# Two inverse-transform row blocks from one PSUM bank each, and the row-block steps listed one by one

## The chip, the cores and the metric

The kernel runs on one core of a Trainium2 chip. The metric is the device time of one execution in microseconds (us). The median of three runs of the kernel before is 1539.2 us (1536.36 to 1539.36). The engines are named PE (matmuls; PEld for its weight loads), DVE (VectorE), ACT (ScalarE), POOL (GpSimd) and SP (SyncE, which issues DMAs).

## What is computed

The state `x` has 2048 rows of 512 columns in bf16. Two layer kinds alternate, twice each:

```python
def _A_ref(x, w_r, w_i):                      # spectral filter
    X = jnp.fft.rfft2(x.astype(jnp.float32), axes=(-2, -1)) * (w_r + 1j * w_i)
    return jnp.fft.irfft2(X, s=(S, D), axes=(-2, -1)).astype(jnp.bfloat16)
...
def _B_ref(x, wq, wk, wv, wo):                # 32 heads share one key and one value, 16 wide
    p = _softmax(scores, axis=-1)             # scores = q k^T / 4
    return (p @ v, heads joined) @ wo
...
x = x + _A_ref(_layernorm(x), A_w_r, A_w_i)
x = x + _B_ref(_layernorm(x), B_wq, B_wk, B_wv, B_wo)
x = x + _A_ref(_layernorm(x), A_w_r, A_w_i)
x = x + _B_ref(_layernorm(x), B_wq, B_wk, B_wv, B_wo)
```

A spectral layer with the attention layer behind it is called a pair here; there are two.

## The kernel before, in words

**Layout.** `x` stays on the chip as `x_sb` of 128 partitions x 4 (r) x 4 (t) x 512. A *block* t is the four rows r = 0..3 of each partition: sequence position 512 r + 4 p + t. One block holds 512 rows of the sequence.

**A pair's stages.** The front normalises the blocks and transforms them along the sequence; `middle` goes over the width, applies the filter and comes back over the width, which leaves the spectra `H` (odd wave numbers) and `G[0]` (even ones). `blocks`, which the change rewrites, does the last inverse transform over the sequence block by block, adds it to `x`, normalises the new rows and makes keys, values and the first queries from them. `run` is then the attention: 579 steps of exponentials on ACT (L672), a part of the exponentials as integer images on DVE and POOL (L706, L721, L725), scores and products on PE (L583, L685).

**The inverse transform of a block.** The four rows of a block at one partition are the sums and differences of two even parts and two odd parts. `odd(t)` (L347) computes the odd parts in a pair of PSUM banks with 16 matmuls and ACT copies them out as `bp` (L354). `even(t, i)` for i = 0, 1 (L365) computes each even part with eight matmuls, both parts in one pair of banks: four with the tables of multiples of four, which are the same for both i, and four with the tables of the other even numbers, which change sign between i = 0 and 1. `rows_out` (L382) adds and subtracts `bp` on DVE. For blocks 2 and 3 (`WITH_X`) PE adds the old `x` through identity matmuls (`old_rows`, L372), so that DVE writes `x_sb` at once; for blocks 0 and 1 DVE writes `dst` and then adds `x` (L384).

**From rows to keys.** `stats_rows` (L115, L119) gives mean and variance per row, `root` (L122) the square root on ACT, `scales` (L126, L127) the factors on DVE, `apply` the normalised rows `X_new` on ACT (L142) or DVE (L144). They reach the layout of the keys, `xz`, either by transposing DMAs on SP (`turned_rows`, L426; two per block, each for two rows) or by eight PE transposes and one copy (`transposed`, L418 and L421). `keys` (L435) then makes a block's keys: ACT casts them (L437) and DVE takes the largest absolute value (L438). `values` (L449) makes values, which ACT writes four times with different factors (L451). `first_queries` (L458), `qabs` (L409) and `ready` (L462 to L464) prepare the first queries with a bound that needs all four largest values.

**What sets the order.** In front, middle and blocks the instructions of PE, ACT and DVE run in the order in which the Python code issues them (`manual_schedule`); a new instruction that needs another engine's result waits on that engine's semaphore, and what stands behind it on its engine waits too. In `blocks` before, the order is: block t's odd and even matmuls, then the `rows_out` of it, with statistics and normalising of block t-1 after the matmuls of block t+1. Blocks 0 and 1 are normalised on ACT and transposed by DMA (four DMAs in a pair), blocks 2 and 3 are normalised on DVE and transposed on PE. A dummy exponential (L1071) loads ACT's table for the attention before the last transposes.

**PSUM.** In this stage three pairs of banks (tag p2) hold the odd and even parts, keys and queries, and two single banks (tag mm) values and transposes. In pair 0 of the kernel before, the single banks are the first to be placed; in pair 1 the pairs are. The attention that follows puts its scores in the first five banks.

Of the kernel before, what the change touches and what calls it, by code (L numbers as in the profile page):

```python
# [12 lines left out]
P = 128  # L13
# [23 lines left out]
WITH_X = (2, 3)  # L37
# [3 lines left out]
def host_tables():  # L41
# [40 lines left out]
    tabs["IE"], tabs["IO"] = bf(ie), bf(io)  # L82
# [108 lines left out]
class Spectral:  # L191
# [149 lines left out]
    def odd(self, t):  # L341
        IO, ps = self.tabs["IO"], self.big()
        for i in range(2):
            for c in range(2):
                h = self.H[:, t % 2, c, :, :]
                for ab in range(2):
                    self.mm(ps[:, i, :], lhsT=IO[:, turned(c, t, ab, i * ab), t, :], rhs=h[:, i ^ ab, :], start=(c == 0 and ab == 0), stop=(c == 1 and ab == 1 and t not in WITH_X))  # L347
# [6 lines left out]
        self.nc.scalar.copy(out=bp_new, in_=ps)  # L354
        self.bp[t] = bp_new

    def even(self, t, i):
        IE = self.tabs["IE"]
        if i == 0:
            self.pair[t] = self.big()  # L360
        ps = self.pair[t]
        for c in range(4):
            for ab in range(2):
                tab = IE[:, 0, 2 * c + ab, t, :] if c < 2 else IE[:, 1, turned(c - 2, t, ab, i), t, :]
                self.mm(ps[:, i, :], lhsT=tab, rhs=self.G[0][:, c, ab, :], start=(c == 0 and ab == 0), stop=(c == 3 and ab == 1 and t not in WITH_X))  # L365
        if t in WITH_X:
            self.old_rows(ps, t, i, False)
# [6 lines left out]
    def rows_out(self, t, us=(0, 1), parts=(slice(0, 2),)):  # L374

        ps, bp, x = self.pair[t], self.bp[t], self.x_sb[:, :, t, :]
        dst = x
        if t not in WITH_X:
            dst = self.work.tile([P, 4, 512], BF, tag="m", bufs=3, name="dst")
        for u in us:  # L380
            for i in parts:
                self.tt(out=dst[:, 2 * u:2 * u + 2, :][:, i, :], in0=ps[:, i, :], in1=bp[:, i, :], op=(ALU.add, ALU.subtract)[u])  # L382
        if t not in WITH_X:
            self.tt(out=x, in0=dst, in1=x, op=ALU.add)  # L384


class Attention:
# [25 lines left out]
    def transposed(self, psum, t, xn, half, engine):  # L413

        ps = psum.tile([P, 2, NC, P], BF, tag="mm", bufs=2)
        for i in range(2):
            for c in range(NC):
                self.nc.tensor.transpose(ps[:, i, c, :], xn[:, 2 * half + i, c * P:(c + 1) * P], self.tabs["EYE"][:, 0, :])  # L418
        k = 4 * t + 2 * half
        copy = engine.copy if engine is self.nc.scalar else engine.tensor_copy  # L420
        copy(out=self.xT[:, k:k + 2, :, :], in_=ps)  # L421
# [6 lines left out]
    def keys(self, psum, t, last=False):  # L428

        nc, aw = self.nc, self.aw  # L430
        k0, k1 = 4 * t, 4 * t + 4
        two = psum.tile([P, 2, 512], F32, tag="p2", bufs=3)
        ps = two[:, 0, 0:(k1 - k0) * P]
        for c in range(NC):
            nc.tensor.matmul(ps, lhsT=aw["wk"][:, c, :], rhs=self.xT[:, k0:k1, c, :],  # L435
                             start=(c == 0), stop=(c == NC - 1))
        cast = lambda: nc.scalar.activation(out=self.KT[:, k0 * P:k1 * P], in_=ps, func=ACT.Identity, bias=self.tabs["KAB"][:, 1:2], scale=self.tabs["KAB"][:, 0:1])  # L437
        bound = lambda: nc.vector.tensor_reduce(out=self.kmax[:, t:t + 1], in_=ps, axis=mybir.AxisListType.X, op=ALU.max, apply_absolute_value=True)  # L438
        if last:
            bound()  # L440
        cast()
        return bound

    def values(self, psum, t):
# [5 lines left out]
        for j in range(4):  # L450
            nc.scalar.mul(out=aw["vaug"][:, j, 4 * t:4 * t + 4, 0:DH], in_=psv, mul=PH_W[j])  # L451
# [7 lines left out]

    def ready(self):  # L460
        nc, kq, qt = self.nc, self.kq, self.QT[0]
        nc.vector.tensor_reduce(out=kq[:, 0:1], in_=self.kmax, axis=mybir.AxisListType.X, op=ALU.max)  # L462
        nc.vector.tensor_scalar(out=kq[:, 1:2], in0=kq[:, 0:1], scalar1=self.tabs["KAB"][:, 2:3], scalar2=self.tabs["KAB"][:, 0:1], op0=ALU.mult, op1=ALU.add)
# [322 lines left out]
def full_kernel(ctx, tc, A_x, A_w_r, A_w_i, B_x, B_wq, B_wk, B_wv, B_wo, out, n_pairs=2):  # L786
# [222 lines left out]
    def blocks(work, sp, psum, att):  # L1009
        A, D = nc.scalar, nc.vector  # L1010

        def put(t, X, engines, rows=range(R)):
            for r, engine in zip(rows, engines):
                norm.apply(engine, x_sb[:, r, t, :], X[:, r, :], r, t)

# [4 lines left out]
        def sums(t):  # L1020
            for i in range(2):
                sp.even(t, i)

        def stats(t, rows=range(R)):
            norm.stats_rows(x_sb[:, :, t, :], t, rows)

        def rows_turned(t, engines):
            norm.scales(t)
            X = new_rows()
            for half in range(2):  # L1030
                put(t, X, engines[2 * half:2 * half + 2], (2 * half, 2 * half + 1))
                att.turned_rows(t, X, half)

        sp.odd(0)
        sums(0)
        sp.rows_out(0, parts=(slice(0, 1), slice(1, 2)))
        sp.odd(1)
        sums(1)
        stats(0)
        norm.root(0)  # L1040
        sp.rows_out(1)
        sp.odd(2)
        sums(2)
        rows_turned(0, (A,) * 4)
        stats(1)
        norm.root(1)
        sp.rows_out(2)
        sp.odd(3)
        sums(3)
        rows_turned(1, (A,) * 4)  # L1050
        bound0 = att.keys(psum, 0)
        stats(2)
        norm.root(2)
        sp.rows_out(3, (0,))
        stats(3, (0, 1))
        norm.root(3, slice(0, 2))
        sp.rows_out(3, (1,))
        norm.scales(2)
        xn2 = new_rows()
        put(2, xn2, (D,) * 4)  # L1060
        att.values(psum, 0)
        norm.scales(3, slice(0, 2))
        xn = new_rows()
        put(3, xn, (D, D), (0, 1))
        att.transposed(psum, 2, xn2, 0, A)
        att.transposed(psum, 2, xn2, 1, A)
        bound1 = att.keys(psum, 1)
        stats(3, (2, 3))
        norm.root(3, slice(2, 4))
        dmyo = small.tile([P, 1], F32, tag="dmyo", bufs=1)  # L1070
        nc.scalar.activation(out=dmyo, in_=norm.eps, func=ACT.Exp)  # L1071
        att.transposed(psum, 3, xn, 0, A)
        query = att.first_queries(psum)
        bound0()
        att.values(psum, 1)
        norm.scales(3, slice(2, 4))
        put(3, xn, (D, D), (2, 3))
        bound1()
        bound2 = att.keys(psum, 2)
        att.transposed(psum, 3, xn, 1, D)  # L1080
        query()
        bound2()
        att.keys(psum, 3, True)
        att.qabs(att.QT[0])
        att.values(psum, 2)
        att.values(psum, 3)

    last, inverse = None, {}
    for pair in range(n_pairs):
        with ExitStack() as es:  # L1090
# [8 lines left out]
            for name in ("IO", "IE"):  # L1099
# [97 lines left out]
```

## Time and profile before

| | us |
|---|---|
| median of three runs | 1539.2 |
| profiled execution, its own time | 1539.34 |
| span in its trace (first to last instruction) | 1537.6 |
| mean granted TensorE clock | 0.984 of full speed |
| pair 0: first sum of the spectra (L339) / first exponential (L672) | 69.77 / 115.49 |
| pair 1: the same | 827.11 / 870.21 |
| pair 0: first `rows_out` of blocks 0, 1, 2, 3 | 79.43, 85.95, 92.47, 98.42 |
| pair 1: the same | 834.98, 841.50, 848.03, 853.98 |

A row of the page's list of groups reads: line, engine, operation, out<-in with partitions x elements and type, xcount | busy us, mean ns of one | idle us of the engine just before, and what ended it. A row of the timeline reads: start, length, engine, line, operation, count, and in brackets the idle time before it with its releaser. The table of stretches gives, for each stretch of time, its length and the busy us (and number) of PE, PEld, DVE, ACT and POOL, then the granted clock of TensorE, the share of the DMA engines and GB/s. The chain of waits lists, in order of time, the work that ended last.

### The profile page before, as it was taken

To read this page: it belongs to the slowest core of one execution; us is meant where nothing else is said; L and a number is where in the kernel's file an instruction comes from. 1 tells how busy PE (TensorE), PEld (TensorE's weight loads), DVE (VectorE), ACT (ScalarE), POOL (GpSimd) and SP (SyncE) were. 2 spreads that over 40 slices of the span, in tenths; PEclk is the share of its full clock that TensorE was granted. 3 is DMA by queue.
4 is the path that set the end of the run, shared out by engine and by line. 5 is a ranking of instruction groups with operands and counts; after the bars stand their busy time and mean duration, and the time that the engine had idled before them with its cause. 6 is when DMAs were issued, how large, how long until landed. Compare 5 with 4: busy or idle time off the path is not lost.

```text
span 1537.6 us, 33033 instructions
## 1 busy us (share of the span) xinstructions
PE 1350.1 (88%) x13181; PEld 432.3 (28%) x13220; DVE 1418.2 (92%) x2273; ACT 1436.7 (93%) x1359; POOL 778.3 (51%) x1310
## 2 busy tenths in 40 slices
PE   5888888899889988999889788888998899889987
PEld 2442222222222222222235322222222222222222
DVE  6688999999999999999987889999999999999996
ACT  6649999999999999999965799999999999999997
POOL 1004555555556555655610055555556655565555
PEclk9997999999999999999999899999999999999999
DMA  8110000000000000000010100000000000000000
GB/s 286 17 28 1 2 2 1 1 1 2 1 2 1 1 1 2 1 2 1 2 42 1 28 1 2 1 1 5 1 5 4 5 5 5 5 4 5 5 5 18
DMA packets 21791, 19.51 MB, mean 13 GB/s; under 512 B 14212, under 2 KB 19076, under 8 KB 21380
## 3 DMA queue, kind: packets, MB, share of 16 engines
q1 hardware_dynamic: 21252, 16.35, 3.5%
q8 instruction: 103, 1.69, 0.5%
q0 software_dynamic: 384, 1.05, 0.2%
q14 instruction: 52, 0.43, 0.1%
HBM read 13.20 MB, written 2.10 MB: 10 GB/s over the span
## 4 chain that ended last, share of the span: by engine, by line
ACT 34%; DVE 34%; issue 14%; PE 14%; POOL 0%; DVEq 0%; POOLq 0%; ACTq 0%
ACT e L672 33%; DVE t_new L706 17%; DVE s_new L721 9%; PE pv_new L685 3%; PE sc L583 3%; PE new L365 2%; DVE o L602 2%; PE new L216 1%; DVE qt L405 1%; DVE ot_new L623 1%; PE dv L583 1%; PE new L347 1%; PE new L255 1%; PE new L311 1%; DVE qt L409 1%
## 5 line engine op out<-in xcount | busy, mean ns | idle before, releaser
L672 ACT ACTIVATE e<-sc 128x1536 bf16<-128x1536 f32 (+1 forms) x1158 | 1313.7, 1298 | 5.4 <-PE dv L583 3.3
L725 POOL TENSOR_SCALAR pool_new<-t_new 128x512 int16<-128x512 int16 x1204 | 727.6, 626 | 717.6 <-DVE s_new L721 629.6
L706 DVE TENSOR_SCALAR t_new<-dv 128x512 uint16<-128x512 f32 x1204 | 790.0, 678 | 58.9 <-PE dv L583 50.7
L685 PE MATMUL pv_new<-e,vaug 128*32 128x512 bf16 x2892 | 586.1, 388 | 0.0
L583 PE MATMUL sc<-qt,KT 32*128 32x512 bf16 x2892 | 457.5, 386 | 117.2 <-ACT e L672 110.6
L583 PE MATMUL dv<-qt,KT 32*128 32x512 bf16 x1204 | 453.2, 386 | 18.7 <-DVE t_new L706 15.7
L685 PE MATMUL pv_new<-s_new,vaug 128*32 128x512 bf16 x2408 | 427.4, 386 | 6.4 <-DVE s_new L721 6.2
L721 DVE TENSOR_SCALAR s_new<-t_new 128x3584 int16<-128x3584 int16 (+1 forms) x380 | 392.8, 1034 | 0.1
L583 PEld LDWEIGHTS <-KT 32*128 32x128 bf16 x4096 | 156.2, 91 | 559.5 <-issue 555.1
L685 PE MATMUL pv_new<-pool_new,vaug 128*32 128x512 bf16 x1204 | 302.2, 385 | 1.3 <-POOL pool_new L725 1.3
L685 PEld LDWEIGHTS <-vaug 128*32 128x32 bf16 x7708 | 156.1, 94 | 379.8 <-issue 348.4
L685 PE MATMUL pv_new<-t_new,vaug 128*32 128x512 bf16 x1204 | 231.2, 385 | 0.3
L399 PE MATMUL ps<-xz,wq_sb 128*128 128x512 bf16 x248 | 65.2, 386 | 1.0 <-DVE t_new L706 0.8
L602 DVE STREAM_TRANSPOSE o<-pv_new 128x512 f32<-128x512 f32 x64 | 45.3, 707 | 7.3 <-PE pv_new L685 7.3
L216 PE MATMUL new<-tab_F,xz 128*128 128x512 bf16 x186 | 48.3, 405 | 3.6 <-DVE xz L180 3.3
L405 DVE TENSOR_SCALAR qt<-ps,kq 128x512 bf16<-128x512 f32 x62 | 46.0, 742 | 1.2 <-PE ps L399 1.2
L617 POOL TENSOR_TENSOR od_new<-o,den 128x256 bf16<-128x256 f32 x62 | 38.4, 620 | 0.0
L115 DVE BATCH_NORM_STATS2 st<-x_sb 128x6 f32<-128x512 bf16 x48 | 31.1, 674 | 3.9 <-DMA x_sb<-in_A_x_dram 3.7
L280 DVE TENSOR_TENSOR m<-x_new,wt 128x1024 bf16<-128x1024 bf16 x32 | 20.7, 688 | 14.3 <-ACT x_new L256 14.3
L256 ACT CAST x_new<-new 128x1024 bf16<-128x1024 f32 x16 | 16.2, 1012 | 18.4 <-PE new L255 17.0
L399 PEld LDWEIGHTS <-wq_sb 128*128 128x128 bf16 x256 | 22.4, 98 | 32.4 <-issue 17.8
L365 PE MATMUL new<-G_new,t_new 128*128 128x512 bf16 x128 | 29.9, 379 | 0.5 <-DVE G_new L332 0.4
(109 smaller groups left out, 586.8 us busy)
## 6 DMA issues: line engine op xcount, KB each, us to landing
tab_F<-const_F SPq DMA_DIRECT2D x5, 640.0 KB, 11.5
x_sb<-in_A_x_dram SPq DMA_DIRECT2D x4, 512.0 KB, 4.8
t_new<-const_IE SPq DMA_DIRECT2D x2, 1024.0 KB
rt<-in_A_w_r_dram SPq DMA_DIRECT2D x1, 1028.0 KB, 7.6
rt<-in_A_w_i_dram SPq DMA_DIRECT2D x1, 1028.0 KB, 11.8
t_new<-const_IO SPq DMA_DIRECT2D x2, 512.0 KB, 5.6
out_dram<-x_sb SPq DMA_DIRECT2D x8, 128.0 KB, 1.7
out_dram<-x_sb POOLq DMA_DIRECT2D x8, 128.0 KB, 2.1
```

Of the source, the lines that this page charges most:

```text
L216: self.mm(ps, lhsT=z, rhs=tab, start=start and i == 0, stop=stop and i == len(mms) - 1)
L365: self.mm(ps[:, i, :], lhsT=tab, rhs=self.G[0][:, c, ab, :], start=(c == 0 and ab == 0), stop=(c == 3 and ab == 1 and t not in WITH_X))
L399: self.nc.tensor.matmul(ps, lhsT=self.aw["wq"][:, c, hg, :], rhs=self.xT[:, 4 * qb:4 * qb + 4, c, :], start=(c == 0), stop=(c == NC - 1))
L405: self.nc.vector.tensor_scalar(out=qt, in0=ps, scalar1=self.kq[:, 1:2], scalar2=None, op0=ALU.mult)
L583: nc.tensor.matmul(dst, lhsT=KT[hs, kc * P:(kc + 1) * P], rhs=QT[g][hs, :], start=True, stop=True)
L602: nc.vector.transpose(out=o.rearrange("p c j -> p (c j)"), in_=ps)
L617: return engine.tensor_tensor(out=turned_od[g // 2][:, :, half], in0=o[:, :, 0:DH], in1=den.unsqueeze(2).broadcast_to([P, 16, DH]), op=ALU ...
L672: nc.scalar.activation(out=e[:, 0:na, :], in_=sc[:, 0:na, :], func=ACT.Exp, scale=SCALE)
L685: nc.tensor.matmul(pv[g][32 * h:32 * h + 32, :], lhsT=vaug[:, max(j, 0), kc, :], rhs=rhs, start=(first_pv[(g, h)] == u), stop=(last_pv[(g, ...
L706: nc.vector.tensor_scalar(out=tb[(g, b)][:, i, :], in0=dv, scalar1=T_MUL, scalar2=T_ADD, op0=ALU.mult, op1=ALU.add)
L721: image[0] = nc.vector.tensor_scalar(out=s_new[:, lo:nt, :], in0=src[:, lo:nt, :], scalar1=PH_OFF[i], scalar2=None, op0=ALU.add)
L725: pace(nc.gpsimd.tensor_scalar(out=sb[(g, b, 3)][:, i, :], in0=src[:, i, :], scalar1=1.0, scalar2=PH_OFF[3], op0=ALU.mult, op1=ALU.add))
```

## The change

1. **Blocks 0 and 1** (`HALVED`): the second even part is no longer computed with eight matmuls in a bank of its own. The first part is computed in one single bank; once DVE has taken its sum and difference with `bp`, four matmuls with a new table `IE2` (minus two times the sign-changing half, 128x3x2x128 bf16, loaded per pair) are added into the same bank, which turns it into the second part. `rows_summed(t, i)` takes sum and difference for one i, `rows_added` adds `x`.
2. **The steps of all four blocks** are issued one by one in a new order: `odd`, `keys` and `values` return their ACT copies as functions that are called later. Block 0's statistics come in two halves, and the DMAs and PE transposes are dealt out anew: blocks 0 and 1 by DMA (four), half of block 2 and half of block 3 by DMA (one each) and the other halves by PE. Block 2 is normalised on ACT, three of block 3's rows on DVE. The dummy exponential comes behind the last transposed copy; the values of blocks 2 and 3 are scaled ahead of the last key cast.
3. **The bound of the queries** is split: `bounds` reduces the first three blocks' largest values, `ready` brings in the fourth with a step that takes the larger of the two.
4. **Bank pairs first**: one unused pair is taken at the start of pair 0, so that the pairs are placed ahead of the single banks, as in pair 1.

```diff
+WITH_X, HALVED = (2, 3), (0, 1)
...
+tabs["IE2"] = bf(2 * ie[:, 1, 1:, :2])
...
     def even(self, t, i):
+        if t in HALVED:
+            if i == 0:
+                self.pair[t] = self.bank()
+            for c in range(2 * i, 4):
+                for ab in range(2):
+                    tab = self.tabs["IE2"][:, turned(c - 2, t, ab, 1) - 1, t, :] if i else IE[...]
+                    self.mm(self.pair[t], lhsT=tab, rhs=self.G[0][:, c, ab, :], start=(c == 0 and ab == 0), stop=(c == 3 and ab == 1), skip_group_check=True)
+            return
...
+    def rows_out(self, t, u):
+        self.tt(out=self.x_sb[:, 2 * u:2 * u + 2, t, :], in0=self.pair[t], in1=self.bp[t], op=(ALU.add, ALU.subtract)[u])
+    def rows_summed(self, t, i):
+        if i == 0:
+            self.dst = self.work.tile([P, 4, 512], BF, tag="m", bufs=3, name="dst")
+        for u in range(2):
+            self.tt(out=self.dst[:, 2 * u + i, :], in0=self.pair[t], in1=self.bp[t][:, i, :], op=(ALU.add, ALU.subtract)[u])
+    def rows_added(self, t, rows=slice(0, R)):
+        x = self.x_sb[:, rows, t, :]
+        self.tt(out=x, in0=self.dst[:, rows, :], in1=x, op=ALU.add)
...
+    def bounds(self):
+        self.nc.vector.tensor_reduce(out=kq[:, 0:1], in_=self.kmax[:, 0:NQB - 1], ...)
+        self.nc.vector.tensor_scalar(out=kq[:, 0:1], in0=kq[:, 0:1], scalar1=kab[:, 2:3], scalar2=kab[:, 0:1], op0=ALU.mult, op1=ALU.add)
     def ready(self):
+        nc.vector.tensor_scalar(out=kq[:, 1:2], in0=self.kmax[:, NQB - 1:NQB], ..., scalar2=kq[:, 0:1], op0=ALU.mult, op1=ALU.max)
...
                 if pair == 0:
+                    sp.big()
                     front_first(work, sp, psum, raw)
```

The new order in `blocks` (ACT is `A`, DVE is `D`):

```python
keep[0] = sp.odd(0); keep[0](); sp.even(0, 0); sp.rows_summed(0, 0); sp.even(0, 1); sp.rows_summed(0, 1)
sp.rows_added(0, slice(1, R, 2)); sp.rows_added(0, slice(0, R, 2)); stats(0, (0, 2))
sp.even(1, 0); keep[1] = sp.odd(1); stats(0, (1, 3)); keep[1](); sp.rows_summed(1, 0)
sp.even(1, 1); norm.root(0); sp.rows_summed(1, 1); keep[2] = sp.odd(2); norm.scales(0)
X[0] = new_rows(); sp.rows_added(1); sp.even(2, 0); put(0, 0, A); stats(1); sp.even(2, 1)
X[1] = new_rows(); put(0, 2, A); keep[3] = sp.odd(3); put(0, 1, A); keep[2](); norm.root(1)
sp.rows_out(2, 0); norm.scales(1); put(0, 3, A); att.turned_rows(0, X[0], 0); sp.even(3, 0)
att.turned_rows(0, X[0], 1); put(1, 0, A); sp.rows_out(2, 1); put(1, 3, A); stats(2, (2, 3)); keep[3]()
put(1, 1, A); sp.even(3, 1); stats(2, (0, 1)); X[2] = new_rows(); norm.root(2)
query = att.first_queries(psum); put(1, 2, A); att.turned_rows(1, X[1], 0); sp.rows_out(3, 0)
norm.scales(2); keys[0] = att.keys(psum, 0); put(2, 1, A); put(2, 2, A); X[3] = new_rows()
stats(3, (0, 1)); put(2, 0, A); put(2, 3, A); turned_out[2, 0] = att.transposed(psum, 2, X[2], 0)
sp.rows_out(3, 1); stats(3, (2, 3)); att.turned_rows(1, X[1], 1); norm.root(3, slice(0, 2))
values[0] = att.values(psum, 0); norm.scales(3, slice(0, 2)); att.turned_rows(2, X[2], 1)
keys[0][0](); norm.root(3, slice(2, 4)); norm.scales(3, slice(2, 4)); put(3, 0, D)
turned_out[2, 0](D.tensor_copy); put(3, 1, A); put(3, 3, D); keys[1] = att.keys(psum, 1)
put(3, 2, D); query(); values[0](); values[1] = att.values(psum, 1); att.turned_rows(3, X[3], 0)
keys[1][0](); values[1](); turned_out[3, 1] = att.transposed(psum, 3, X[3], 1); turned_out[3, 1](A.copy)
table_loaded(); keys[0][1](); keys[2] = att.keys(psum, 2); keys[1][1](); att.qabs(att.QT[0])
keys[3] = att.keys(psum, 3); keys[2][1](); att.bounds(); values[2] = att.values(psum, 2); keys[2][0]()
values[3] = att.values(psum, 3); values[2](); keys[3][1](); values[3](); keys[3][0]()
```

More of the change, by code (lines that the diff above doesn't have):

```diff
@@ L419, in transposed @@
         k = 4 * t + 2 * half
[L420 to L421 removed]
+        return lambda copy: copy(out=self.xT[:, k:k + 2, :, :], in_=ps)
     def turned_rows(self, t, xn, half):
@@ L1018, in new_rows, with put @@
             return X_new
-        def sums(t):
-            for i in range(2):
-                sp.even(t, i)
+        def put(t, r, engine):
+            norm.apply(engine, x_sb[:, r, t, :], X[t][:, r, :], r, t)
         def stats(t, rows=range(R)):
             norm.stats_rows(x_sb[:, :, t, :], t, rows)
[L1027 to L1032, printed above, removed]
@@ new lines, in blocks @@
+        X, keep, keys, values, turned_out = {}, {}, {}, {}, {}
+        keep[0] = sp.odd(0)
+        keep[0]()
+        sp.even(0, 0)
+        sp.rows_summed(0, 0)
+        sp.even(0, 1)
+        sp.rows_summed(0, 1)
+        sp.rows_added(0, slice(1, R, 2))
+        sp.rows_added(0, slice(0, R, 2))
+        stats(0, (0, 2))
+        sp.even(1, 0)
+        keep[1] = sp.odd(1)
+        stats(0, (1, 3))
+        keep[1]()
+        sp.rows_summed(1, 0)
+        sp.even(1, 1)
+        norm.root(0)
@@ new lines, in blocks @@
+        sp.rows_summed(1, 1)
+        keep[2] = sp.odd(2)
+        norm.scales(0)
+        X[0] = new_rows()
+        sp.rows_added(1)
+        sp.even(2, 0)
+        put(0, 0, A)
+        stats(1)
+        sp.even(2, 1)
+        X[1] = new_rows()
+        put(0, 2, A)
+        keep[3] = sp.odd(3)
+        put(0, 1, A)
+        keep[2]()
+        norm.root(1)
+        sp.rows_out(2, 0)
+        norm.scales(1)
+        put(0, 3, A)
+        att.turned_rows(0, X[0], 0)
+        sp.even(3, 0)
+        att.turned_rows(0, X[0], 1)
@@ new lines, in blocks @@
+        put(1, 0, A)
+        sp.rows_out(2, 1)
+        put(1, 3, A)
+        stats(2, (2, 3))
+        keep[3]()
+        put(1, 1, A)
+        sp.even(3, 1)
+        stats(2, (0, 1))
+        X[2] = new_rows()
+        norm.root(2)
+        query = att.first_queries(psum)
+        put(1, 2, A)
+        att.turned_rows(1, X[1], 0)
+        sp.rows_out(3, 0)
+        norm.scales(2)
+        keys[0] = att.keys(psum, 0)
+        put(2, 1, A)
+        put(2, 2, A)
+        X[3] = new_rows()
+        stats(3, (0, 1))
@@ L1088, in full_kernel @@
+        keys[2][1]()
+        att.bounds()
+        values[2] = att.values(psum, 2)
+        keys[2][0]()
+        values[3] = att.values(psum, 3)
+        values[2]()
+        keys[3][1]()
+        values[3]()
+        keys[3][0]()
     last, inverse = None, {}
```

121 lines of the change are left out of this document (47 added, 74 removed).

## The prediction

> **What bounds the kernel now.** I read the page first: the span and the busy shares.
>
> ```profile
> span 1537.6 us, 33033 instructions
> PE 1350.1 (88%) x13181; PEld 432.3 (28%) x13220; DVE 1418.2 (92%) x2273; ACT 1436.7 (93%) x1359; POOL 778.3 (51%) x1310
> L672 ACT ACTIVATE e<-sc 128x1536 bf16<-128x1536 f32 (+1 forms) x1158 | 1313.7, 1298 | 5.4 <-PE dv L583 3.3
> ```
>
> Most of the span is the exponentials of the two attention stages, which this change leaves alone. What it rewrites lies between the last inverse step and the first exponential of each layer pair (first exponentials at 115.49 and 870.21 us). So the second view is a table of the stretches inside these two windows: us of PE, PEld, DVE, ACT, POOL busy, then the granted TensorE clock.
>
> ```profile
> 76.50:98.40 21.90, 21.72 (x100) 9.91 (x102) 18.24 (x39) 9.38 (x13) 0.00 (x0) 1.00 0.15 30
> 98.40:115.50 17.10, 11.08 (x123) 7.12 (x122) 13.53 (x34) 9.82 (x29) 0.00 (x0) 0.80 0.14 26
> 831.10:854.00 22.90, 22.78 (x105) 10.31 (x106) 19.22 (x41) 10.39 (x14) 0.00 (x0) 1.00 0.18 29
> 854.00:870.20 16.20, 10.51 (x122) 6.38 (x122) 13.51 (x34) 9.77 (x28) 0.00 (x0) 0.88 0.14 26
> ```
>
> Two parts, then. In the **rows part** PE has no idle time to speak of (21.72 of 21.90), and DVE is close behind (18.24). In the **tail** no engine is full; a chain through DVE, PE and ACT sets the time. The chain of waits says the same: unbroken PE pieces up to 98.3, then DVE.
>
> ```profile
> 76.57 2.75 PE new L365 x12
> 79.32 1.73 PE new L347 x8
> 81.05 3.45 PE new L365 x16
> ...
> 97.89 0.45 PE new L372 x2
> ...
> 98.42 1.24 DVE x_sb L382
> 99.68 1.29 DVE st L115 x2
> ...
> 114.09 0.92 ACT vaug L451 x8
> ```
>
> A saving on PE there shortens the span only if PE gets no new wait. So the third view is the order of the changed program's instructions with what each waits for. I laid that order out in time: each instruction starts when its engine is free and the last thing it waits for is done, with durations of the rows of before grouped by shape. 512-column matmuls (L365, L347, L372) are 0.2155 us apart (8 in 1.73) and take 0.38; DVE reads of a 128x512 bank take 0.68, 0.60 apart (L382, four in 2.48); a 128x1024 bf16 sum takes 0.69, 0.61 apart (L331, L332); statistics are 0.60 apart (L115); L382 on 128x1024 takes 1.21. The same laying out of before puts the first exponentials at 114.8 and 869.7, so it is 0.7 and 0.5 us early; the half clock seen below is why.
>
> **The rows part.** *Removed:* blocks 0 and 1 need 12 even matmuls instead of 16: 2 x 4 x 0.2155 = 1.72 us of PE per pair. *Added:* the second row accumulates into the bank of the first, so its four matmuls must wait until DVE has read the first row twice; PE works in order, and all its later matmuls queue behind them.
>
> Block 0: the first row's last matmul starts at 77.19 and ends at 77.57. DVE reads it from 77.61 to 78.89. PE, free at 77.40, resumes at 78.95: stall 1.54. Then 4+8+8 matmuls keep it busy until 83.26.
> Block 1: its four matmuls wait for DVE's two reads of block 1's first row, and DVE has before them: two reads of block 0's second row (from 80.01), two 128x1024 sums, four statistics with their aggregates (2.78). The reads run from 85.44 to 86.72; PE resumes at 86.78: stall 3.52.
> Sum: 1.54 + 3.52 - 1.72 = +3.34. From 86.8 PE runs gapless to the last L372 matmul, so `rows_out` of block 3 starts at 101.63 rather than 98.42 (+3.2). In pair 1 the same steps give 857.17 rather than 853.98.
>
> **The tail.** Laid out from 101.63: three stretches of DVE (two `rows_out` of 1.1 to 1.2, statistics, scales) until 107.78; two normalised rows, the copy of block 2's transposed half and another two rows, as the order has them (0.33+0.60+0.33+0.41) until 109.45; eight transposes until 110.24; the ACT copy, 0.91 to the next; the table load (1.28 in row L1071) and its dummy until 112.58; key cast 0.68, eight scaled values 0.83, last key cast 0.78 until 114.87; three score matmuls; first exponential at 115.77. That is 14.14 us, against 17.07 and 16.23 in the trace. The tail gains 2.9 and 2.1, because block 2's four rows are normalised on ACT beside block 3's `rows_out` instead of on DVE behind it, and because PE has 16 transposes in it instead of 32. So with a full clock everywhere: pair 0 115.77 - 115.49 = +0.28, pair 1 871.31 - 870.21 = +1.10; **+1.4 in sum**. Pair 1 gains less since its first scores today run beside ACT's last scaled values; with the last key cast last on ACT, and the scores waiting for it, 0.85 is bare.
>
> **The clock.** The two idle stretches of PE in today's tails are as long as the new stall:
>
> ```profile
> 103.08 0.71 PE L418 MATMUL ps<-tab_EYE,X_new 128*128 128x128 bf16 x5 [3.52 <-DVE X_new L144]
> ```
> ```profile
> 98.30:101.70 3.40, 1.26 (x21) 0.74 (x18) 3.24 (x6) 1.44 (x6) 0.00 (x0) 1.00 0.68 128
> 101.70:108.50 6.80, 5.42 (x31) 3.60 (x32) 5.90 (x20) 3.97 (x8) 0.00 (x0) 0.50 0.02 4
> 115.40:125.60 10.20, 8.64 (x53) 1.90 (x49) 7.48 (x11) 9.14 (x8) 1.48 (x3) 0.50 0.01 2
> 859.50:862.80 3.30, 3.30 (x21) 2.02 (x18) 3.00 (x10) 2.66 (x4) 0.00 (x0) 0.50 0.00 0
> ```
>
> After idle times of 3.52 and 3.51 the granted clock (the third number from the end) was 0.50 for 6.8 and 3.3 us, with matmuls 0.43 apart. A 3.52 stall ahead of 14.5 us in which PE alone sets the pace costs half of what the half clock covers. The rows show the state kept for 3.4 or 6.8 us. Let the drop come at any point of such a 3.4 us grid: for some 2.5 of the 3.4 us the stretch before it holds most of the stall and the clock falls, between 85.5 and 88; 3.4 us of it, less what falls on the stall, then cost 1.1 to 1.7, and 6.8 us up to 3.4. The mean over the grid, with the sparse PE of the new tail, is about 1.2 a pair: **2 x 1.2 = +2.4**, ends 0 and 6.1 for both pairs.
>
> [...]
>
> **Costed at nothing.** The new table (192 KB a pair, behind IE's 1024 KB on SP's queue; 0.7 us at the 286 GB/s of the first slice) loads tens of us before its use; uncovered it costs 0.7. Transposing DMAs go from four to six a pair; on SP's queue nothing else moves then. The last is issued at 108.29 and lands 3.2 later (median of xz<-X_new) at 111.49, when the last keys' matmuls are due; it has 0.8 of slack before the last key cast, beyond that each us costs one. The split of the largest-key reduction adds one tiny DVE step and hides under the values. Placing the bank pairs first gives pair 0 the bank order that pair 1 has: the first scores wait for the last of ACT's work as before (115.06 after L451). Both ends of these: -0.3 to +0.8.
>
> **Sum:** 1539.34 (profiled execution; span 1537.6 and 1.7 around it; the median of the runs shown is 1539.2) + 1.4 + 2.4 = 1543.1, taken as **1543.0**.
>
> **Rivals.**
> *A, stalls, but a full clock* (chance 0.25): the idle time falls so that no half clock follows, or it ends before PE's long stretch. For it: the drop depends on where the idle time lies; 1.72 us of idle at 113.3 were followed by 0.50, 2.01 at 789 were not. Against it: both idle times of 3.5 were. Time 1539.3 + 1.4 = 1540.7. Not slower by what can be told.
> *B, the loop's beginning gains the clock* (0.10): today the clock is also 0.50 at 115.4 to 125.6 and again later, and the exponentials' pace, 6.72 for six, falls to 7.95 and 7.52 there; I count 2.3 us lost in pair 0 and 1.6 in pair 1. If the new tail's shorter idle times (2.2 and 1.5) keep the clock full until the loop is running, these come back: 1540.7 - 3.9 = 1536.8, faster than before. It decides from the point where the last 3.4 us before the first scores hold enough matmuls; the layout has only sparse ones there, which speaks against it.
> *C, the half clock lasts and the tail slips too* (0.10): both pairs lose the full 6.8 us window and the last DMA lands late: 1539.3 + 1.4 + 6.1 + 0.8 = 1547.6.
> *D, the stalls don't arise* (0.05), because DVE reads are quicker than rows of before say. Then PE ends 1.7 earlier instead of 3.2 later, about 5 a pair less than A: near 1531.
> The forecast keeps 0.50.
>
> **Numbers.** 0.2% (3.1 us) is about what a measurement of this kernel can tell from no change. The forecast's own spread, 1541 to 1545, lies mostly but not all above 1542.3: of its 0.50, 0.38 slower and 0.12 the same. A adds 0.22 same and 0.03 slower; B 0.06 same and 0.04 faster; C 0.09 slower and 0.01 same; D 0.05 faster. Faster 0.09, same 0.41, slower 0.50. The range reaches from between A and B to C's lower part: 1538.5 to 1547.
>
> **What would show it.** Right: PE idle near 1.5 and 3.5 us before the last four even matmuls of blocks 0 and 1, released by DVE's reads of the bank; a granted clock of 0.50 soon after; first exponentials some 1.5 and 2.4 us later than 115.49 and 870.21 counted from the inverse step; a tail of 14 to 15 us from block 3's first `rows_out`. Wrong: no PE idle in the rows part (D), clock 1.00 throughout it (A), or exponentials at 6.72 for six from the start (B).

## The result, and the profile after

The changed kernel takes 1545.62 us (median of five runs, 1543.77 to 1545.76) against 1537.84 for the kernel before beside it (1536.36 to 1539.36): a ratio of 1.0046, 95% interval 1.0031 to 1.0061. It is slower by 7.8 us between the medians, beyond the 0.2% that can be told.

The profiled execution of the changed kernel took 1543.77, the fastest of its five; the profiled one of before, on which the prediction was built, took 1539.34, near the upper end of all runs of before. So the two traces show 4.4 of the 7.8 us. The page first, its span, its busy shares and the row of the exponentials (L686 now):

```profile
span 1542.0 us, 32956 instructions
PE 1343.6 (87%) x13133; PEld 427.0 (28%) x13172; DVE 1416.6 (92%) x2271; ACT 1440.7 (93%) x1365; POOL 778.3 (50%) x1310
L686 ACT ACTIVATE e<-sc 128x1536 bf16<-128x1536 f32 (+1 forms) x1158 | 1314.0, 1301 | 5.6 <-PE dv L597 3.3
```

PE is busy for 6.5 us less, the exponentials are what they were, and the span is 4.4 longer. The loss is idle time, and the table of stretches says where (columns as before: length; PE, PEld, DVE, ACT, POOL busy; granted clock). The rows part and the tail of pair 0, then those of pair 1:

```profile
76.50:102.10 25.60, 20.34 (x92) 9.13 (x94) 19.23 (x42) 9.71 (x15) 0.00 (x0) 1.00 0.15 29
102.10:117.60 15.50, 9.35 (x107) 5.08 (x106) 12.02 (x30) 11.41 (x30) 0.00 (x0) 0.85 0.42 57
833.00:860.30 27.30, 22.37 (x96) 9.71 (x97) 19.67 (x43) 10.54 (x15) 0.00 (x0) 0.94 0.14 27
860.30:874.40 14.10, 8.01 (x107) 4.52 (x106) 12.01 (x30) 11.40 (x30) 0.00 (x0) 0.99 0.39 62
```

PE had no idle time in the rows part (21.72 of 21.90); now it has 5 us of it (20.34 of 25.60). The timeline of PE names what it waits for (start, length, line, operation; in brackets the idle time before it), two stalls in pair 0 and the same two in pair 1:

```profile
79.33 2.75 PE L366 MATMUL new<-G_new,t_new 128*128 128x512 bf16 x12 [1.45 <-DVE dst L392]
...
87.16 1.02 PE L366 MATMUL new<-G_new,t_new 128*128 128x512 bf16 x4 [3.35 <-DVE dst L392]
```
```profile
836.27 2.75 PE L366 MATMUL new<-G_new,t_new 128*128 128x512 bf16 x12 [1.45 <-DVE dst L392]
...
844.10 1.87 PE L366 MATMUL new<-G_new,t_new 128*128 128x512 bf16 x4 [3.35 <-DVE dst L392]
```

L392 is `rows_summed`: PE waits until DVE has read the shared bank. The last of these lines shows the clock as well. The same four matmuls take 1.02 us in pair 0 and 1.87 in pair 1, where the granted clock was 0.50 from 843.31 to 846.73 (the third number from the end):

```profile
839.90:843.31 3.41, 0.85 (x4) 0.29 (x3) 3.38 (x10) 1.31 (x2) 0.00 (x0) 1.00 0.00 0
843.31:846.73 3.42, 2.63 (x7) 0.97 (x7) 1.46 (x4) 0.00 (x0) 0.00 (x0) 0.50 0.00 0
```

The new tail has one more stall, which the chain of waits of pair 0 shows (start, length, what):

```profile
108.01 0.80 ACT X_new L142
108.81 0.07 ACT vaug L459
108.88 4.75 DMA xz<-X_new
113.63 0.14 issue
113.76 1.02 PE two L445 x4
```

The last transposing DMA is 4.75 us on the path. In before no DMA stands in the chain here. The timeline shows what waits for it in pair 0, and then in pair 1, where it lands 3.04 after its issue: the last keys' matmuls on PE and, behind them, the eight scaled values of blocks 2 and 3 on ACT.

```profile
113.76 1.02 PE L445 MATMUL two<-xz,wka 128*128 128x512 bf16 x4 [2.11 <-DMA xz<-X_new]
115.21 1.04 ACT L459 ACTIVATE vaug<-psv 128x64 bf16<-128x64 f32 x8 [1.32 <-PE psv L455]
...
870.70 1.02 PE L445 MATMUL two<-xz,wka 128*128 128x512 bf16 x4 [0.83 <-DMA xz<-X_new]
872.15 1.04 ACT L459 ACTIVATE vaug<-psv 128x64 bf16<-128x64 f32 x8
```

To compare kernels, each pair is cut in two: from the first sum of the spectra (L339) to block 3's first `rows_out` (the rows part with the end of the inverse step), and from there to the first exponential (the tail). The traces of all the kernels told of below, in us:

| kernel | rows, pair 0 | tail, pair 0 | rows, pair 1 | tail, pair 1 | span |
|---|---|---|---|---|---|
| before | 28.65 | 17.07 | 26.87 | 16.23 | 1537.57 |
| before_same | 28.66 | 17.19 | 26.86 | 16.39 | 1537.49 |
| after | 32.05 | 15.51 | 31.54 | 14.13 | 1541.99 |
| after_same | 33.73 | 15.49 | 31.54 | 14.32 | 1543.02 |
| halved_old | 30.15 | 16.93 | 28.36 | 16.33 | 1538.20 |
| two_banks | 28.65 | 15.87 | 26.87 | 14.52 | 1534.34 |
| fill2 | 29.46 | 16.38 | 27.68 | 14.90 | 1536.44 |
| warm | 32.05 | 15.14 | 30.26 | 14.01 | 1539.03 |
| no_first_pair | 33.73 | 14.69 | 31.94 | 14.42 | 1541.75 |
| t3pe | 33.74 | 14.33 | 32.30 | 15.02 | 1542.23 |
| two_t3pe | 28.65 | 14.54 | 27.24 | 14.85 | 1533.22 |
| two_kt2 | 28.66 | 14.66 | 26.86 | 13.67 | 1531.19 |
| two_kt2_t3pe | 28.65 | 13.77 | 27.23 | 13.76 | 1529.83 |
| two_kt2_nofirst | 28.66 | 14.16 | 26.86 | 14.33 | 1532.19 |

Outside these stretches the traces differ too (start of pair 0 68.56 to 70.14, the exponentials of pair 0, from the start of the first to that of the last, 658.2 to 660.5, of pair 1 656.3 to 657.3). Stretches of clock 0.50 fall differently at the beginning of these loops (in pair 0 115.4 to 125.6 in before, 116.3 to 129.9 in after), which may be a part of it. It is the scatter of single traces; the medians carry the verdicts.

### The profile page after: what moved, and what is told of

The parts are those of the page before. It is cut to its first block, busy times and chain, and to the rows that moved or that the text cites. A ratio compares the mean times of both kernels' runs of the same rounds, so it can differ in the third digit from the quotient of the medians.

```text
span 1542.0 us, 32956 instructions
## 1 busy us (share of the span) xinstructions
PE 1343.6 (87%) x13133; PEld 427.0 (28%) x13172; DVE 1416.6 (92%) x2271; ACT 1440.7 (93%) x1365; POOL 778.3 (50%) x1310
## 4 chain that ended last, share of the span: by engine, by line
ACT 35%; DVE 35%; issue 14%; PE 13%; DMA 1%; POOL 0%; DVEq 0%; POOLq 0%; ACTq 0%
ACT e L686 33%; DVE t_new L720 17%; DVE s_new L735 9%; PE sc L597 3%; PE pv_new L699 3%; DVE o L616 1%; PE new L216 1%; DVE qt L417 1%; DVE ot_new L637 1%; PE dv L597 1%; PE new L374 1%; PE new L255 1%; DVE st L115 1%; PE new L311 1%; PE new L347 1%
## 5 line engine op out<-in xcount | busy, mean ns | idle before, releaser
L686 ACT ACTIVATE e<-sc 128x1536 bf16<-128x1536 f32 (+1 forms) x1158 | 1314.0, 1301 | 5.6 <-PE dv L597 3.3
L142 ACT ACTIVATE X_new<-x_sb,ln_nb,ln_rstd 128x512 bf16<-128x512 bf16 x26 | 19.8, 805 | 16.4 <-DVE ln_nb L127 16.4
```

What stands on the lines that cost most here:

```text
L686: nc.scalar.activation(out=e[:, 0:na, :], in_=sc[:, 0:na, :], func=ACT.Exp, scale=SCALE)
```

## The experiments

Theory: the sharing of the bank costs PE two stalls a pair, with a half clock behind the longer one; the new order of the steps by itself is a gain. Rivals: the new order is what costs; or the clock alone, without the bare length of the stalls.

**1. A bank for each even part** (two_banks). The changed kernel, but blocks 0 and 1 compute each even part with eight matmuls in a single bank of its own, so that nothing accumulates into a bank that DVE reads. The new table is still loaded, unused.

```diff
-            if i == 0:
-                self.pair[t] = self.bank()
-            for c in range(2 * i, 4):
+            self.pair[t] = self.bank()
+            for c in range(4):
...
-                    tab = self.tabs["IE2"][...] if i else IE[:, 0, 2 * c + ab, t, :] if c < 2 else IE[:, 1, turned(c - 2, t, ab, 0), t, :]
+                    tab = IE[:, 0, 2 * c + ab, t, :] if c < 2 else IE[:, 1, turned(c - 2, t, ab, i), t, :]
```

> The changed kernel with its new order of steps, but blocks 0 and 1 compute their second even part with eight matmuls in a single bank of its own again (the new table is loaded and not used). Theory (PE waits for DVE's reads of the shared bank, net +3.3 us a pair, and a half clock after the 3.4 us stall comes on top; the new tail is 2 to 3 us shorter than the old): PE has no idle time over 0.5 us in the rows part, block 3's first rows_out comes 3.3 us earlier than in the changed kernel in each pair, first exponentials at least 3.3 earlier; median 1534 to 1539, so 6.7 to 11 below the changed kernel's 1545.6. Rival 1 (the new order of steps itself costs the time): within 2 us of the changed kernel. Rival 2 (only the half clock costs): 1541 to 1543, and the rows part as long as in a changed kernel with a full clock.

Measured 1534.34 (1533.25 to 1536.15), ratio to before 0.9977 (0.9968 to 0.9987): faster than before, some 11 us below the changed kernel. PE's timeline at the same place:

```profile
76.94 4.48 PE L365 MATMUL new<-G_new,t_new 128*128 128x512 bf16 x20 [0.41 <-DVE G_new L332]
81.25 1.89 PE L347 MATMUL new<-H_new,t_new 128*128 128x512 bf16 x8
82.98 1.89 PE L365 MATMUL new<-G_new,t_new 128*128 128x512 bf16 x8
```

No wait for L391 or L392 is left, and the rows part takes 28.65 and 26.87, to a hundredth what it took before. The new order is innocent; with it and without the shared bank the kernel is faster than before. All of the loss comes with the sharing of the bank, which leaves out eight matmuls a pair.

**2. The shared bank alone** (halved_old): before's order and DMAs, with `even` halved and DVE reading part by part.

```diff
-        sums(0)
-        sp.rows_out(0, parts=(slice(0, 1), slice(1, 2)))
+        for i in range(2):
+            sp.even(0, i)
+            sp.rows_summed(0, i)
+        sp.rows_added(0)
...
-        sums(1)
+        sp.even(1, 0)
+        sp.rows_summed(1, 0)
+        sp.even(1, 1)
...
```

> The kernel before with the shared bank alone: blocks 0 and 1 compute their second even part by four matmuls in the bank of the first, with DVE's reads between; the order of all later steps, the DMAs and the bank placement are those of before. Theory: 1.72 us of matmuls saved against stalls of 1.5 and 3 us that are laid out by the same rows: first exponentials 1.35 later than before in each pair, with a full clock or with the clock's usual share, so 1540 to 1542 against 1537.8. Rival 1 (the order of steps is the cost, the bank is free): 1536 to 1538, below or at before.

Measured 1541.01 (1539.65 to 1541.49), ratio 1.0017 (1.0009 to 1.0026). The rows part is 1.50 longer in both pairs, the tail is the old one (16.93 and 16.33). Here block 1's stall is as short as block 0's:

```profile
79.23 1.02 PE L366 MATMUL new<-G_new,t_new 128*128 128x512 bf16 x4 [1.45 <-DVE dst L400]
...
85.16 1.02 PE L366 MATMUL new<-G_new,t_new 128*128 128x512 bf16 x4 [1.45 <-DVE dst L400]
```

The bound is in the rows: two stalls of 1.45, each counted from the end of the last matmul, which is 0.17 later than PE was free (0.38 - 0.2155), less 1.72 of matmuls: 2 x 1.62 - 1.72 = 1.52. Halving loses with a full clock too, because what it saves (1.72) is shorter than the wait that it makes (3.24); the granted clock was 1.00 over its rows part in pair 0 (76.5 to 100.1).

**3. Work in the stall** (fill2): the changed kernel with block 2's odd matmuls moved ahead of the waiting ones.

```diff
+        keep[2] = sp.odd(2)
         sp.even(1, 1)
         norm.root(0)
         sp.rows_summed(1, 1)
-        keep[2] = sp.odd(2)
```

> The changed kernel with one step moved: block 2's twelve odd matmuls are issued ahead of block 1's last four even ones, so that they run in PE's second stall; the shared banks stay. Theory: 12 x 0.2155 = 2.6 us of the 3.4 us stall are filled, the half clock after it is gone, first exponentials 2.6 earlier than in the changed kernel in each pair; median 1536 to 1540. Rival 1 (order of the tail costs): within 2 us of the changed kernel, since the tail is untouched. Rival 2 (only the half clock): 1541 to 1543.

Measured 1537.26 (1536.07 to 1538.28), ratio 0.9995 (0.9986 to 1.0004): as fast as before, 8 below the changed kernel. The long stall is 0.76 instead of 3.35:

```profile
86.48 0.81 PE L366 MATMUL new<-G_new,t_new 128*128 128x512 bf16 x3 [0.76 <-DVE dst L392]
```

**4. The clock by itself** (warm): the changed kernel, with eight matmuls that compute half of block 0's odd part once more, for nothing, ahead of the waiting ones. They end before DVE does, so that PE resumes at the same point, after 1.62 us of idle time instead of 3.35:

```profile
86.09 1.02 PE L373 MATMUL new<-G_new,t_new 128*128 128x512 bf16 x4 [1.62 <-DVE dst L399]
```

```diff
         keep[1] = sp.odd(1)
+        sp.odd_again(0)
```

> The changed kernel with eight useless matmuls added: block 0's odd part is computed a second time into its own banks, after it was copied out, ahead of block 1's last four even matmuls. They fill half of the second stall and move no other step, so they tell the half clock from the stall. Theory: the stall's end and block 3's first rows_out stay where they are with a full clock, only the half clock in the rows part goes (1.2 us a pair on average, up to 3); pair 0 also loses 0.85 because the first scores get another bank that doesn't wait for the last key cast; median 1541 to 1544. Rival 2 (the clock is the whole loss): 1537 to 1539. Rival 1 (order): 1545.

Measured 1539.73 (1538.57 to 1542.03), ratio 1.0010 (1.0001 to 1.0019): eight more matmuls a pair make the changed kernel some 5.7 faster. The median lies below what the theory expected (1541 to 1544) and just above what rival 2 did (1537 to 1539), so the traces have to decide. In the traces of before and of the changed kernel the changes of the clock lie whole multiples of 3.41 us apart, so the time is cut here into windows of that length (more on this under 5). The window that holds the stall and the one behind it, for pair 0 of warm and then for a second profile of the changed kernel (after_same, below):

```profile
83.55:86.97 3.42, 1.79 (x10) 0.70 (x8) 2.48 (x6) 0.53 (x2) 0.00 (x0) 1.00 0.00 0
86.97:90.38 3.41, 3.36 (x16) 1.54 (x16) 3.16 (x6) 1.56 (x3) 0.00 (x0) 1.00 0.00 0
```
```profile
82.44:85.86 3.42, 0.20 (x1) 0.10 (x1) 3.17 (x9) 1.22 (x2) 0.00 (x0) 1.00 0.00 0
85.86:89.27 3.41, 3.41 (x9) 1.21 (x8) 1.83 (x5) 0.20 (x1) 0.00 (x0) 0.50 0.00 0
```

In the second window PE has no idle time to speak of in either, but it issues 16 matmuls in warm and 9 in the changed kernel. In pair 1 warm's stall lies in one window as well (1.85 of 3.41 us busy), and the clock stayed at 1.00 (840.0 to 846.8). Warm's rows part takes 32.05 and 30.26: the full-clock length, 3.40 and 3.39 above before. So the clock is 1.68 of the loss in pair 0 of after_same (33.73) and 1.28 in pair 1 (31.54), and the rival that it is all of the loss falls: with a full clock the rows parts are still 6.8 longer than those of before, and warm is near before only because its tails (15.14 and 14.01) are 4.2 shorter. Rows and tails together put warm 3.6 below after_same, and the profiled executions are 4.0 apart (1540.81 and 1544.80); the medians are 5.7 apart, and what the runs that were not profiled have beyond that was not seen.

**5. The changed kernel again** (after_same), for a second trace and five more runs.

> The changed kernel itself again, so that the others of this chip stand beside it. Theory: as far above before as on the first chip, 1543 to 1546; the shared bank's two waits of PE in each pair (1.4 and 3.3 us), with or without a half clock after the second, and in pair 0 the last transposing DMA again held up, because 16 KB of instructions are fetched while it runs.

Measured 1545.45 (1544.80 to 1545.71), ratio 1.0047 (1.0034 to 1.0060). It shows why the half clock was missing in pair 0 of the first trace. The changes of the clock within these traces lie whole multiples of 3.413 us apart (in the first trace 106.03 and 843.31, 216 windows; in before 101.70 and 859.46, 222), so the borders can be counted back to a stall that no change follows. In the first trace the same stall of 3.35 us fell across the border at 85.56, and was left half in each window:

```profile
82.14:85.56 3.42, 1.67 (x8) 0.68 (x7) 3.38 (x8) 1.01 (x1) 0.00 (x0) 1.00 0.00 0
85.56:88.97 3.41, 1.81 (x9) 0.86 (x9) 2.29 (x7) 0.30 (x1) 0.00 (x0) 1.00 0.00 0
```

With 1.67 of 3.42 busy the clock stayed at 1.00; with 0.20 (above) it was 0.50 in the next window. In pair 1 of the first trace 0.85 of 3.41 were busy from 839.90 to 843.31, and it was 0.50 behind that too. Busy time alone does not tell these outcomes apart, though. In the tail of the first trace, where 32 of the 36 matmuls of a window are of 16 columns, 1.81 of 3.41 were busy and the next window was at 0.50:

```profile
112.86:116.27 3.41, 1.81 (x36) 1.27 (x37) 1.59 (x4) 2.08 (x12) 0.00 (x0) 1.00 0.01 1
116.27:119.69 3.42, 1.96 (x12) 0.54 (x13) 1.59 (x3) 2.71 (x3) 0.00 (x0) 0.50 0.00 0
```

**6. The last DMA** (t3pe and two_t3pe): block 3's first half is turned by eight PE transposes and a DVE copy, in the changed kernel and in two_banks.

```diff
-        att.turned_rows(3, X[3], 0)
+        turned_out[3, 0] = att.transposed(psum, 3, X[3], 0)
+        turned_out[3, 0](D.tensor_copy)
```

> The kernel with two banks and the new order (two_banks), with block 3's first half turned by eight PE transposes and a DVE copy instead of the last transposing DMA. Two theories of pair 0's first exponential, which came 1.9 us later after the inverse step than laid out while pair 1's came 0.5 later. Theory D (the last DMA is held up by the instruction fetch): pair 0's stretch from the first sum of the spectra to the first exponential falls from 44.5 to some 43.5, pair 1's rises by the 0.5 that the PE transposes and the copy cost; in sum 0 to 1.5 less, 1533 to 1535. Rival (the half clock in the tail makes pair 0 late, the DMA lands when it must): both pairs 0.5 longer, 1535 to 1536.

> The changed kernel with block 3's first half turned by eight PE transposes and a DVE copy instead of the last transposing DMA. Laid out, this costs 0.46 a pair (first exponentials 116.22 and 871.76 instead of 115.76 and 871.30). Theory that the slipped last DMA of pair 0 costs about 1.6: 1545.5 + 0.9 - 1.6 = 1544.8, no wait for a DMA ahead of the last keys, pair 0 about 1 shorter, pair 1 about 0.5 longer. Rival, that the slip is hidden in most executions: 1546.4, 0.9 above the changed kernel.

Measured 1534.53 (1534.06 to 1535.69), ratio 0.9979 (0.9970 to 0.9988), against two_banks' 0.9977; and 1545.05 (1543.72 to 1546.03), ratio 1.0045 (1.0032 to 1.0057), against 1.0047 and 1.0046. Neither difference can be told from none by its interval. The traces go the way of the theory: pair 0's tail falls from 15.5 to 14.33 and from 15.87 to 14.54, though the layout makes it 0.46 longer, and pair 1's tail, where the DMA was not late, grows from 14.1 to 15.02 and from 14.52 to 14.85. Taken with the layout's 0.46, the late DMAs cost an estimated 1.6 to 1.8 in pair 0 of these traces. Replacing the last one gives much of that back in pair 1, where in two_t3pe also the rows part is 0.37 longer (27.24 for 26.87; 0.18 of it is a wait of block 0's even matmuls for DVE's L332).

**7. The order of the last casts** (two_kt2): two_banks with the last two key casts ahead of the scaled values of blocks 2 and 3.

```diff
-        values[2]()
         keys[3][1]()
-        values[3]()
         keys[3][0]()
+        values[2]()
+        values[3]()
```

> two_banks with the last keys' bound and cast issued on ACT ahead of the scaled values of blocks 2 and 3, since the first scores wait for that cast (it frees their banks). Theory: the scores run beside the eight scaled values, 0.75 earlier in each pair, 1.5 in sum: 1532 to 1534. Rival (the last DMA holds the keys so late that the cast can't come earlier): nothing in pair 0, 0.75 in pair 1: 1533 to 1534.5, and ACT idle ahead of the cast.

Measured 1533.32 (1532.96 to 1535.54), ratio 0.9971 (0.9960 to 0.9983). The tails are 14.66 and 13.67, 1.2 and 0.85 shorter than those of two_banks. In pair 0 not all of it is the order: PE waits 0.40 for the last two transposing DMAs where it waited 1.53 in two_banks. The medians, on two chips, differ by less than the intervals.

**8. Without the unused bank pair** (no_first_pair in the changed kernel, two_kt2_nofirst in two_kt2): the `sp.big()` at the start of pair 0 is left out.

> The changed kernel without the unused bank pair at the start of pair 0, so that the single banks are placed first there as in before. Theory: the first scores of pair 0 then wait for the last scaled values instead of the last key cast, 0.65 earlier; pair 1 as it is; 0 to 1 less than the changed kernel on this chip. Rival (placing the pairs first gains time elsewhere, which this gives back): 1 or more above the changed kernel.

> The version with a bank for each even part and the last key casts ahead of the scaled values, without the unused bank pair at the start of pair 0. Laid out, pair 0 loses 0.86 (112.52 instead of 111.66), because the first scores then wait for a bank that ACT reads late; pair 1 is unchanged. By the layout 1533.3 + 0.9 = 1534.2. Rival: leaving the pair out gained 2.0 in the changed kernel where the layout gave 0.65; if that was another effect of the bank order, it gains here too: 1532 or less.

Measured 1543.46 (1542.33 to 1544.33), ratio 1.0035 (1.0023 to 1.0048), 2.0 below after_same on the same chip; and 1533.37 (1532.16 to 1534.00), ratio 0.9970 (0.9958 to 0.9982), the same as two_kt2. In the changed kernel the trace shows 0.80 of it in pair 0's tail (15.49 to 14.69): the first scores start beside the last key cast instead of behind it. The whole is more than was expected (0 to 1), and the remainder is not in that stretch. Neither expectation for two_kt2_nofirst came true (a loss of 0.9, a gain of over 1). What the bank order is worth beyond 0.8 stays open.

**9. The two together** (two_kt2_t3pe).

> The version with a bank for each even part and the last key casts ahead of the scaled values (1533.3), with block 3's first half turned by PE instead of the last DMA. Laid out +0.52 a pair (112.18 and 867.72 instead of 111.66 and 867.20). If a late last DMA is a cost there too (its packets were stretched in pair 0), the sum is 1533.3 + 1.0 - 1.3 = 1533.0, the same; if not, 1534.3.

Measured 1533.56 (1531.63 to 1533.59), ratio 0.9967 (0.9954 to 0.9979): the same as two_kt2. These versions beat both kernels, by 0.3% and 0.75%.

**10. The kernel before again** (before_same), for the spread of its runs.

> The kernel before again, for a second profile of it: its executions spread over 1536 to 1539.7, and the profiled one on which the prediction was built took 1539.34. Theory: the spread is the half clock in the two tails falling in different 3.4 us windows, so an execution near 1536.5 shows fewer or shorter rows of 0.50 between 100 and 147 and between 859 and 897, and first exponentials 1 to 1.5 us earlier in sum over both pairs, the rest of the trace alike. Rival: the spread comes from the front or the loops; then the stretches from the first sum to the first exponential stay within 0.3 of 45.72 and 43.09.

The profiled execution took 1539.26, again near the upper end, so it does not answer the question: no execution near 1536.5 was seen in a trace. What the runs alone show is that time and mean granted clock go together: 1536.4 to 1537 at 0.988 to 0.990, 1538.9 to 1539.4 at 0.985.

## Why the prediction was right, and where its sizes were off

**The rows part** was right to 0.2 us. Removed: 1.72. Added: stalls of 1.54 and 3.52 counted from the moment that PE is free; measured idle 1.45 and 3.35 from the end of the last matmul, 1.62 and 3.52 counted as in the prediction. Sum +3.34 forecast, +3.2 at block 3's first `rows_out`; measured +3.40 in pair 0 of the first trace and, by warm's trace, +3.39 in pair 1.

**The clock** was right in kind (0.50 behind the long stall in three of the four cases of the two traces) and near in its size. Forecast 1.2 a pair as a mean over the grid, and 1.1 to 1.7 where the clock falls for 3.4 us; measured 0 and 1.28 in the first trace, 1.68 and 1.28 in the second, a mean of 1.06. Against the 2.4 of the sum that is 1.28 and 2.96. The prediction's picture of the grid, by which the place of the stall decides, is what the two traces show. It is one kernel and one stall of 3.35 with two outcomes: laid across the border at 85.56, with 1.67 and 1.81 us of PE busy in the two windows, it was followed by a clock of 1.00; where it left 0.20 busy in the window up to 85.86, by 0.50. The window ahead of a half clock need not be idle: in pair 1 of the first trace PE was busy for 0.85 of its 3.41. The prediction's own row of before says the same: the idle time of 3.52 lay across the border at 101.70, and 1.26 of the 3.40 us ahead of it were busy.

**The tail** was right in pair 1: 14.14 forecast, 14.13 measured. In pair 0 it was 15.51, and the step that failed is one of those costed at nothing: "The last is issued at 108.29 and lands 3.2 later ... it has 0.8 of slack". It was issued at 108.88 and landed 4.75 later. The prediction had such a slip only in rival C. The slack was mis-sized too. It was counted to the last key cast, but the eight scaled values stand ahead of that cast on ACT, and their matmuls stand behind the last keys' on PE: in both pairs they start 1.58 after the landing. In pair 1, with a landing after 3.04, ACT has no idle time to speak of ahead of them, so there was no slack. In pair 0 the idle time is 1.32, nearly all of the 1.37 by which the tail is above the forecast.

**The base** was too high. The sum was made against the profiled execution's 1539.34, with the median of three runs beside it (1539.2). With all the runs the median of before is 1537.5 to 1538.7. So the number 1543.0 has two errors that partly cancel: terms that add up to 3.8 where the medians differ by 7.8, and a base that was 1.5 too high. That it lies only 2.6 below the measured 1545.6 is in part luck. By the stretches of the first trace the terms add up to 4.4: against the forecast's 3.8 the rows are 0.4 more, the clock 1.1 less and the tails 1.4 more. By those of the second they add up to 6.3: 0.4, 0.6 and 1.5 more. The two traces of after lie 1.85 and 0.65 below the median of their own runs, the one of before lies 1.5 above, and what the other runs of after have beyond the traces was not seen.

**The rivals.** A (full clock) held in pair 0 of the first trace and not in the second; its time, 1540.7, leaves out the DMA. B (the loop's beginning gains the clock) fell: the rows of 0.50 at the beginning of the loops are still there in after (116.3 to 129.9 and 874.0 to 884.3), and the loops take 660.0 and 656.8 against 660.5 and 656.6. C came half true: the DMA was late, but behind the stalls the clock was 0.50 for one window of 3.41 (843.31 to 846.73 in the first trace of after, 85.86 to 89.27 in the second) and not for 6.8. D (no stalls) fell. The measured 1545.6 lies just above the forecast's own spread (1541 to 1545), below C's 1547.6.

## What to carry to other kernels

Accumulating into a bank that DVE had still to read made PE wait 1.45 and 3.35 us a pair here, to save 1.72. In no run here did the sharing pay: with the long stall filled by other matmuls (fill2, 0.76 instead of 3.35) the loss was gone, and with a bank for each part (two_banks) there was a gain of 0.23%. Before sharing a bank, look for work that PE can do ahead of the waiting matmuls and that lasts as long as the reads queued before them. Where PE sets the pace, price an idle stretch like this one of 3.35 us twice: its length, and the half clock that may follow (in the two traces of after it cost 0, 1.28 or 1.68, by where the stall lay). Count the slack of a transfer to the first instruction that waits for it through any engine, not to the last. And build the sum on a trace whose time stands at the median of several runs, not on the one execution that was profiled.

## What the runs showed of the hardware

**Transposing DMAs beside instruction transfers.** The view of DMAs has one row for each queue; the share times the window times 16 engines over the packets is the mean time of a packet. The first window of the changed kernel holds block 2's transposing DMA, alone (77.4% of 1.8 us, 21 ns a packet); the second holds the last one, with a 16 KB transfer on the instruction queue from 111.11 to 112.24 (104.3% of 3.2 us, 51 ns):

```profile
q1 hardware_dynamic: 1056, 0.26, 77.4%
```
```profile
q1 hardware_dynamic: 1056, 0.26, 104.3%
q8 instruction: 1, 0.02, 2.2%
```

The packets of the first take 1.42 us from beginning to end, those of the second 3.02. The mean hides how: in both windows half of the packets take 18 ns or less, and in the second 36 of the 1056 make up 32.7 of the 53.4 us. The same view's rate in 40 slices, of 0.08 us each, shows two gaps, near 111.0 and from 111.6 on:

```profile
GB/s 32 128 211 211 237 198 218 179 154 74 38 10 6 243 246 285 259 272 285 81 0 0 0 0 0 0 0 3 10 6 10 6 10 10 10 10 13 26 3 0
```

In pair 1 of the same trace the 16 KB transfer (865.56 to 866.64) meets block 2's DMA instead, which takes 1.86 us and 33.5 ns a packet; the last one, without such a transfer, takes 1.41 us and 21 ns. In pair 0 of after_same, fill2 and no_first_pair the last DMA meets it and takes 3.0 us from beginning to end (56, 56 and 27 ns a packet). In pair 0 of warm, two_banks, two_kt2 and two_t3pe it is block 2's (47, 52, 35 and 40 ns), and in warm and two_banks the last one begins only where that one ends. In pair 0 of t3pe the DMAs have ended before the transfer begins, and the last takes 1.42. In pair 0 of before it comes at 105.06, when all four DMAs have ended. That the instruction transfer is the cause is argued from this coincidence; no run moved it by itself. It does not account for all of it: in after 19 packets wait from 110.55 to 111.11, ahead of the transfer's beginning, and the last packets end 0.8 behind its end.

**A half clock that hides.** In after_same the clock was 0.50 from 106.34 to 113.16, in the first trace only from 106.03 to 109.45, yet pair 0's tail is the same (15.49 and 15.51), since the last keys' matmuls wait for the late DMA in both: they start 0.70 and 0.69 after its last packet. (The trace of after_same puts their wait down to DVE's L472, but the program issues that behind them.) In the rows part, where PE sets the pace, 3.4 us at 0.50 cost 1.28 to 1.68. Here the slow clock had a price only where nothing else was later.
